# Attention and mixer: the last 64 keys' scores and a quarter of each diagonal score block turned by DMA, turns queued by the slot that needs them

## The chip, the cores and the metric

The kernel runs on one core of a Trainium2 chip. The metric is device time in microseconds (us) of the whole program, the median of the runs; lower is better. PE is the matrix engine, ACT, DVE and POOL are the scalar, vector and GpSimd engines, and SP is the engine whose queue issues all DMAs here.

## What is computed

For each of 8 batches, with S = 3136 positions, D = 256 and d_qk = 64:

```
scores = (1/S) * z @ z.T                      # S x S
x      = u * (max(scores, 0)**2 @ v)          # S x D
x2     = x + (x.T @ U @ V).T                  # rank 32
out    = x2 + max(x2 @ w_ch1, 0) @ w_ch2      # hidden 1024
```

Scores come from z with itself, so the score matrix is symmetric. The kernel works in bf16 with sums in float32.

## The kernel before

**Tiles and groups.** The 3136 positions are 24 full tiles of 128 (NF) and a tail of 64. Four tiles make a group (GT = 4, GW = 512 columns); a batch has 6 full groups (NQ) and the tail as a seventh "group" of 64 (NG = 7). `zzTs[b]` holds z transposed, twice, in the upper and the lower 64 rows, so that a score matmul contracts over 64 rows and two matmuls run side by side, one in each half of the array's rows. Nearly all matmuls come in such pairs (`pair`, line 164, called at line 169).

**Score blocks.** `blocks[b, g, J]` is a tile of 128 keys x 4 key tiles x 512 query columns: the squared, rectified scores of key group J against query group g. It is made by two "jobs" (h = 0 and 1), each a pair of 512-column matmuls (`score_pairs`, line 359), one rectification of 1024 columns (`rectify`, lines 327 to 336, on ACT or DVE, whichever the planner thinks free first) and one square on DVE (line 325). Only blocks with J >= g are made so. A block with J < g is the transpose of another one: `issue_turn` (line 346) has a DMA turn it from SBUF to SBUF (line 351, a "turn"). In batch 0 some blocks are made twice instead of turned (`made_twice`: g up to FIRST = 3, or J = g - 1). Twenty block buffers (NBLK) are shared by score blocks, turned blocks, hidden activations and some loads; `take_block` and `give_block` hand them round.

**The last 64 keys.** The 64 keys of the tail against the 512 queries of two groups are one more job, "last" (three a batch): a pair of 512-column matmuls, a rectification and a square into `last_sb`, which `av_end` (line 609) uses as the last weights of an attention sum. The opposite piece, all keys against the 64 tail queries, is made by `score_small` (line 426) into `attn_small`, in the slot of the batch's last full group, and used by `av_small` (line 562).

**Slots.** The program is one list of 56 slots t = b * 7 + g (the loop at line 1104). In slot t PE sums attention for (b, g) over its six blocks in the order J = 0 to 5 (`av_stream`), makes the scores of later slots (`todo`, line 1083; the jobs of a group are made one slot ahead, those of a new batch over three slots), and does the mixer for the group of seven slots before: `u2_unit` (line 672, the rank-32 part), the turn of x into `u2T` by DMA (`x_turn`, line 631, DMA at line 634), and, one slot later, the hidden layer (`ch1_part`, line 770, reading `u2T`; `ch2_stream`, line 812).

**The planner.** The order of all instructions is written out at build time. A modelled clock (`clock`, in units of a pair of 256 columns) advances with the matmuls, and `free_at` holds when ACT, DVE and SP are thought to be free. `held` is a list of actions with due times; `run_held` (line 114) runs those that are due. A finished square puts a block's turn into `ready_turns`; whenever SP is thought free (`free_at["sp"] <= now`) and no first group's x waits (`urgent`), the turn with the smallest (J, b, g) is issued. Each DMA books time on SP: 34 units a block turn, 15/512 a KB for a plain transfer, 17/256 for a turned one.

All DMAs stand in SP's one queue, in order. `lhs` (line 512) is what an attention matmul asks for its weights: a block made directly is read in its own layout, a turned block in another; if a turn isn't issued yet, it is issued there.

Of the kernel before, what the change touches and what calls it, by code (L numbers as in the profile page):

```python
# [9 lines left out]
BF16 = mybir.dt.bfloat16  # L10
# [8 lines left out]
def kernel(  # L19
# [79 lines left out]
    unturned = {}  # L99
    ready_turns = []  # L100
    urgent = []

    def book(eng, ready, cost):
        free_at[eng] = max(free_at[eng], ready) + cost
# [21 lines left out]
    def pe(cost):  # L126
        clock[0] += cost
# [192 lines left out]
    def half(zzT, jj, c0, n):  # L320
        return zzT.rearrange("p t c -> p (t c)")[jj * dqk : (jj + 1) * dqk, c0 : c0 + n]

    def square(a, cost=6.3):
        book("dve", clock[0], cost)
        nc.vector.tensor_tensor(out=a, in0=a, in1=a, op=ALU.mult)  # L325

    def rectify(dst, src):

        ready = clock[0] + 3
        if max(free_at["dve"], ready) + 8 < max(free_at["act"], ready):  # L330
            nc.vector.tensor_scalar(  # L331
                out=dst, in0=src, scalar1=scale, scalar2=0.0, op0=ALU.mult, op1=ALU.max
            )
            return book("dve", ready, 11.2)
        nc.scalar.activation(out=dst, in_=src, func=AF.Relu, scale=scale)  # L335
        return book("act", ready, 8.7)

# [5 lines left out]
    def made_twice(b, g, J):  # L343
        return b == 0 and (g <= FIRST or J == g - 1)

    def issue_turn(e):
# [4 lines left out]
        nc.sync.dma_start_transpose(  # L351
            out=blocks[b, J, g][1].rearrange("p j (q c) -> p (j q) c", c=P),
            in_=src[1].rearrange("p j c -> p (j c)"),
        )
        book("sp", clock[0], 34)
        if unturned.pop(src[0]):
            free_blocks.append(src[0])

    def score_pairs(jobs):

        made = []
        for b, g, job in jobs:
            zzT = zzTs[b]
            k, ps = take_ps()
            if job == "last":
# [4 lines left out]
            pair(  # L370
                k,
                [
                    (
                        jj,
                        jj,
                        dict(
                            out=ps[:, jj, :],
                            lhsT=half(zzT, jj, keys[jj] * P, P),
                            rhs=half(zzT, jj, cols[jj], GW),
                            start=True,  # L380
                            stop=True,
                        ),
                    )
                    for jj in range(2)
                ],
                GW,
            )
            if job == "last":
                lasts[b, g // 2] = pool.tile([P, 2, GW], BF16, name="last_sb")
                made.append((lasts[b, g // 2], k, ps, None, None))  # L390
                continue
            if h == 0:
                blocks[b, g, J] = take_block()
            made.append(
                (
                    blocks[b, g, J][1][:, 2 * h : 2 * h + 2, :],
                    k,
                    ps,
                    (J, g, b) if h == 1 and J > g and not made_twice(b, J, g) else None,
                    (b, g, J),  # L400
                )
            )
        return made

    def score_finish(made):
        for dst, k, ps, turn, key in made:
            if turn:
# [12 lines left out]
            hold(done, finish)  # L420

    def score_burst(jobs):
        score_finish(score_pairs(jobs))


    def score_small(b, g):
        zzT = zzTs[b]
# [6 lines left out]
        for p0 in range(0, npair, per):  # L434
            n = min(per, npair - p0)
            pk, ps = take_ps()
            for k in range(n):
                pair(
                    pk,
                    [  # L440
                        (
                            jj,
                            jj,
                            dict(
                                out=ps[:, jj, k * gw : (k + 1) * gw],
                                lhsT=half(zzT, jj, (2 * (p0 + k) + jj) * P, P),
                                rhs=half(zzT, jj, g0, gw),
                                start=(k == 0),
                                stop=(k == n - 1 and (jj == 1 or p0 + n < npair)),
                            ),  # L450
                        )
                        for jj in range(2)
                    ],
                    gw,
                )
            made.append((p0, n, pk, ps))
# [54 lines left out]
    def av_stream(b, g, box):  # L511
        def lhs(h, q, jt):
            jb, j = divmod(jt, GT)
            while (b, jb) not in v_cast:
                if spare and not b:
                    spare.pop(0)()
                else:
                    run_held(min(h[0] for h in held))
            while (b, g, jb) not in blocks:
                if (g, jb, b) in ready_turns:  # L520
                    issue_turn((g, jb, b))
                else:
                    run_held(min(h[0] for h in held))
            t = blocks[b, g, jb][1]
            if jb >= g or made_twice(b, g, jb):
                while squared.get((b, g, jb), 0) < 2:
                    run_held(min(h[0] for h in held))
                return t[h, j, q * P : (q + 1) * P]

            return t.rearrange("p a c -> p (a c)")[h, (q * GT + j) * P : (q * GT + j + 1) * P]  # L530
# [31 lines left out]
    def av_small(b, g):  # L562
# [3 lines left out]
        for jt in range(NT):  # L566
            c = jt % 2
            for h in range(2):
                nc.tensor.matmul(  # L569
                    out=ps[c * hp : c * hp + rows, h, :D],  # L570
                    lhsT=smalls[b][h * hp : (h + 1) * hp, jt, :],
                    rhs=v_bfs[b][h * hp : (h + 1) * hp, jt, :],
                    start=(jt < 2),
                    stop=(jt >= NT - 2),
                    tile_position=(h * hp, c * hp),
                )
# [31 lines left out]

    def av_end(b, g, box):

        last = lasts[b, g // 2]
        for a in range(2):
            pair(
                box["k"],
# [2 lines left out]
                    a,  # L617
                    lambda h, q: dict(
                        out=four(box["ps"])[:, q, :],
                        lhsT=last[h, g % 2, q * P : (q + 1) * P],  # L620
                        rhs=v_bfs[b][h, NF, :],
                        start=False,
                        stop=(a == 1),
# [460 lines left out]
    for b in range(B):  # L1084
        for g in range(NQ):
# [7 lines left out]
                todo[t + 1] += new[12:] if b == 1 else []  # L1093
            elif b == 0 and g == 0:
                todo[0] += new[4:]
            else:
                todo[t] += new

# [3 lines left out]

    direct = (B - 1, 0)
    for t in range(n_items):
        att = items[t]
        u2i = items[t - NG] if t >= NG else None
        mix = items[t - NG - 1] if t > NG else None
# [166 lines left out]
```

## Time and profile before

| what | value |
|---|---|
| median of 3 runs | 1004.55 us (1003.33 to 1005.26) |
| the profiled execution | 1002.76 us, its span 1001.0 us |
| granted TensorE clock | 1.000 |
| PE, DVE, ACT busy | 984.9, 655.9, 520.3 us |
| q1, the DMA queue: share of 16 engines | 77.1% |
| HBM read, written | 62.56, 25.69 MB |

The span runs from the first to the last instruction. A busy time is the time in which the engine executes at least one instruction. In a group's row, "x" stands before the count, then come the busy time in us, the mean ns of one, the idle time of the engine just before these instructions and what ended it. In a row of waits stand who waited, for whom, the total in us, how often and the longest. In a timeline row stand the start in us, the length, the engine, the line and the operation, and a count. SPq is SP's queue; its DMA rows tell how long SP took to issue.

### The profile page before, as it was taken

To read this page: it belongs to the slowest core of one execution; us is meant where nothing else is said; L and a number is where in the kernel's file an instruction comes from. 1 tells how busy PE (TensorE), PEld (TensorE's weight loads), DVE (VectorE), ACT (ScalarE), POOL (GpSimd) and SP (SyncE) were. 2 spreads that over 40 slices of the span, in tenths; PEclk is the share of its full clock that TensorE was granted. 3 is DMA by queue.
4 is the path that set the end of the run, shared out by engine and by line. 5 is a ranking of instruction groups with operands and counts; after the bars stand their busy time and mean duration, and the time that the engine had idled before them with its cause. 6 is when DMAs were issued, how large, how long until landed. Compare 5 with 4: busy or idle time off the path is not lost.

```text
span 1001.0 us, 35345 instructions
## 1 busy us (share of the span) xinstructions
PE 984.9 (98%) x16179; PEld 820.1 (82%) x16179; DVE 655.9 (66%) x822; ACT 520.3 (52%) x597; POOL 16.6 (2%) x24
## 2 busy tenths in 40 slices
PE   6999999999999999999999999999999999999997
PEld 4898888877888788887888878888888877787776
DVE  6986856668566776666856677566775667653453
ACT  6896843457335473345643465435653356522453
POOL 4100000000000000000000000000000000000000
PEclk9999999999999999999999999999999999999999
DMA  8997898978886799877897789976889586863142
GB/s 260 197 252 177 188 182 182 196 164 190 168 205 137 177 174 183 191 129 183 157 217 166 141 179 176 198 170 139 182 186 194 142 170 143 154 126 89 45 104 95
DMA packets 337061, 167.84 MB, mean 168 GB/s; under 512 B 312336, under 2 KB 315408, under 8 KB 336912
## 3 DMA queue, kind: packets, MB, share of 16 engines
q1 hardware_dynamic: 336912, 165.59, 77.1%
q8 instruction: 126, 2.06, 0.9%
q14 instruction: 23, 0.19, 0.1%
HBM read 62.56 MB, written 25.69 MB: 88 GB/s over the span
## 4 chain that ended last, share of the span: by engine, by line
PE 94%; DVE 3%; ACT 2%; issue 0%; DMA 0%; POOLq 0%; ACTq 0%
PE ps L169 92%; DVE blk L325 1%; PE ps L569 1%; ACT blk L810 1%; PE ps L646 1%; DVE out_sb L719 1%; ACT blk L335 1%; PE ps L861 0%; DMA blk<-in_z_dram 0%; DVE blk L331 0%; DVE blk L847 0%; DVE blk L1065 0%; DVE x_bf L602 0%; PE ps L306 0%; ACT zzT L315 0%
## 5 line engine op out<-in xcount | busy, mean ns | idle before, releaser
L169 PEld LDWEIGHTS <-blk 64*128 64x128 bf16 x12288 | 647.6, 94 | 123.6 <-POOLq L159 8.7
L169 PE MATMUL ps<-v_bf,blk 64*128 64x256 bf16 x9216 | 620.4, 269 | 3.3 <-DVE blk L325 2.8
L335 ACT ACTIVATE blk<-ps 128x1024 bf16<-128x1024 f32 x334 | 333.1, 1027 | 330.3 <-PE ps L169 328.5
L325 DVE TENSOR_TENSOR blk<-blk 128x1024 bf16<-128x1024 bf16 x352 | 237.3, 700 | 34.1 <-ACT blk L335 33.3
L169 PE MATMUL ps<-u2T,w_bf 64*128 64x512 bf16 (+1 forms) x1792 | 240.7, 349 | 0.7
L807 DVE TENSOR_SCALAR blk<-ps 128x1024 bf16<-128x1024 f32 (+1 forms) x114 | 132.1, 1159 | 96.1 <-PE ps L169 95.2
L169 PE MATMUL ps<-w_bf,blk 64*128 64x256 bf16 x3072 | 194.1, 269 | 0.2
L169 PE MATMUL ps<-zzT 64*128 64x512 bf16 (+1 forms) x944 | 144.9, 341 | 2.3 <-ACT zzT L315 1.7
L810 ACT ACTIVATE blk<-ps 128x1024 bf16<-128x1024 f32 (+1 forms) x110 | 93.4, 859 | 82.7 <-PE ps L169 75.2
L169 PEld LDWEIGHTS <-w_bf 64*128 64x128 bf16 x1792 | 95.8, 94 | 27.4 <-POOLq L159 3.0
L602 DVE TENSOR_TENSOR x_bf<-ps,u_sb 128x1024 bf16<-128x1024 f32 x48 | 58.7, 1222 | 62.0 <-PE ps L169 61.9
L719 DVE TENSOR_TENSOR out_sb<-ps,x_bf 128x1024 f32<-128x1024 f32 (+1 forms) x49 | 54.2, 1107 | 51.1 <-PE ps L169 50.8
L847 DVE TENSOR_TENSOR out_sb<-ps,out_sb 128x1024 f32<-128x1024 f32 x42 | 51.3, 1222 | 18.3 <-PE ps L169 18.3
L169 PEld LDWEIGHTS <-zzT 64*128 64x128 bf16 x944 | 46.1, 95 | 8.4 <-issue 2.6
L335 ACT ACTIVATE last_sb<-ps 128x1024 bf16<-128x1024 f32 x23 | 23.6, 1024 | 28.4 <-PE ps L169 28.4
L169 PE MATMUL ps<-t_sb,V_bf 64*128 64x256 bf16 x200 | 21.1, 269 | 0.0
L331 DVE TENSOR_SCALAR blk<-ps 128x1024 bf16<-128x1024 f32 x14 | 17.1, 1224 | 5.6 <-PE ps L169 4.8
L191 DVE CAST v_bf<-stage 128x1024 bf16<-128x1024 f32 (+1 forms) x30 | 20.0, 670 | 0.0
L191 DVE CAST x_bf<-out_sb 128x1024 bf16<-128x1024 f32 x28 | 19.3, 690 | 0.5
L169 PE MATMUL ps<-v_bf,last_sb 64*128 64x256 bf16 x192 | 18.8, 269 | 0.0
L847 DVE TENSOR_TENSOR blk<-ps,blk 128x1024 f32<-128x1024 f32 x6 | 7.3, 1225 | 16.0 <-PE ps L169 15.9
L588 ACT COPY u_sb<-ps 64x512 f32<-64x512 f32 x8 | 4.7, 582 | 23.9 <-PE ps L569 23.9
(68 smaller groups left out, 255.7 us busy)
## 6 DMA issues: line engine op xcount, KB each, us to landing
u_sb<-in_u_dram SPq DMA_DIRECT2D x48, 512.0 KB, 5.1
stage<-in_v_dram SPq DMA_DIRECT2D x42, 512.0 KB, 6.0
out_dram<-out_sb SPq DMA_DIRECT2D x42, 512.0 KB, 3.1
stage<-in_z_dram SPq DMA_DIRECT2D x7, 512.0 KB, 5.4
blk<-in_v_dram SPq DMA_DIRECT2D x6, 512.0 KB, 6.2
out_dram<-blk SPq DMA_DIRECT2D x6, 512.0 KB, 2.6
blk<-in_moe_w_ch_dram SPq DMA_DIRECT2D x4, 512.0 KB, 4.9
stage<-in_z_dram SPq DMA_DIRECT2D x7, 256.0 KB, 5.7
```

What stands on the lines that cost most here:

```text
L169: ins = nc.tensor.matmul(**args)
L191: nc.vector.tensor_copy(out=out, in_=in_)
L325: nc.vector.tensor_tensor(out=a, in0=a, in1=a, op=ALU.mult)
L331: nc.vector.tensor_scalar(out=dst, in0=src, scalar1=scale, scalar2=0.0, op0=ALU.mult, op1=ALU.max)
L335: nc.scalar.activation(out=dst, in_=src, func=AF.Relu, scale=scale)
L569: nc.tensor.matmul(out=ps[c * hp : c * hp + rows, h, :D], lhsT=smalls[b][h * hp : (h + 1) * hp, jt, :], rhs=v_bfs[b][h * hp : (h + 1) * hp ...
L602: nc.vector.tensor_tensor(out=xs[b, g][:rows, :n, :], in0=four(box["ps"])[:rows, :n, :], in1=u_sbs[b, g][:rows, :n, :], op=ALU.mult,)
L646: nc.tensor.matmul(out=pt[c * R : (c + 1) * R, 0, :D], lhsT=U_bf[:rows, it, :], rhs=xs[b, g][:rows, q, :], start=(it < NREP), stop=(it + N ...
L719: nc.vector.tensor_tensor(out=o[:rows, :n, :], in0=four(ps)[:rows, :n, :], in1=x, op=ALU.add)
L807: nc.vector.tensor_single_scalar(out=r, in_=ps[:, :, :gw], scalar=0.0, op=ALU.max)
L810: nc.scalar.activation(out=r, in_=ps[:, :, :gw], func=AF.Relu)
L847: nc.vector.tensor_tensor(out=o, in0=acc, in1=o, op=ALU.add)
```

## The change

1. **Last keys by DMA.** For batches 1 to 7 the "last" jobs go. Instead `score_small` for batch b runs one batch earlier (in slot 5 of batch b - 1; for batch 0 in slot 4), and at the start of the batch's first slot `last_turn` turns the first 24 tiles of `attn_small` (128 x 1536) into `last_sb` (128 x 12 x 128) with one DMA. `place_of` permutes the key tiles in `attn_small` within a group so that the two halves of rows of `last_sb` hold the query tiles that they are used for. `last_sb` has one buffer in place of two. Batch 0 keeps its three "last" jobs; those of groups 2 and 4 move one slot later.
2. **A quarter of diagonal blocks by DMA.** For blocks with J = g (in batch 0 only for g = 4 and 5) the second job is made for the second 256 query columns alone, and a DMA turns the missing quarter (128 x 512) out of the first job's half, within the same block. `in_split` finds the pieces in the new layout, and `lhs` asks for the quarter turn before the weights that need it are read. The new DMA is queued as a turn is.
3. **The order and the figures of turns.** `ready_turns` is sorted by the slot that needs the block (`needed`), and a turn that is needed in this slot or the next may be issued up to 30 units before SP is thought free. The booked figures shrink: 30 units a block turn, 12/512 and 15/256 a KB; a half rectification is booked at 6.4 or 5.3, a half square at 3.7, a quarter turn at 12, a last turn at 26.

```diff
 def queued(kb, turned=False):
-        book("sp", clock[0], kb * (17 / 256 if turned else 15 / 512))
+        book("sp", clock[0], kb * (15 / 256 if turned else 12 / 512))
...
-        while ready_turns and free_at["sp"] <= now and not urgent:
-            issue_turn(min(ready_turns, key=lambda e: (e[0], e[2], e[1])))
+        while ready_turns and not urgent:
+            e = min(ready_turns, key=needed)
+            if free_at["sp"] > now + (30 if needed(e)[0] <= slot[0] + 1 else 0):
+                break
+            issue_turn(e)
...
+    def split(b, g, J):
+        return J == g and not (b == 0 and g <= FIRST)
...
+    def in_split(j, q):
+        if j < 2:
+            return (q // 2 * 2 + j) * hw + q % 2 * P
+        return 2 * GW + (j - 2) * hw + (q - 2) * P if q >= 2 else 3 * GW + (q * 2 + j - 2) * P
...
     def issue_turn(e):
         ready_turns.remove(e)
         J, g, b = e
         src = blocks[b, g, J]
+        if J == g:
+            nc.sync.dma_start_transpose(
+                out=flat_of(src)[:, 3 * GW :].rearrange("p (n c) -> p n c", c=P),
+                in_=flat_of(src)[:, GW : 2 * GW],
+            )
+            book("sp", clock[0], 12)
+            split_turned.add((b, g))
+            return
...
-        book("sp", clock[0], 34)
+        book("sp", clock[0], 30)
...
                 keys, cols = [J * GT + 2 * h + jj for jj in range(2)], [groups[g][0]] * 2
+                if split(b, g, J) and h:
+                    width = hw
+                    cols = [c + hw for c in cols]
...
+    def last_turn(b):
+        lasts[b] = last_tile()
+        nc.sync.dma_start_transpose(
+            out=lasts[b], in_=smalls[b][:, :NF, :].rearrange("p t c -> p (t c)")
+        )
+        book("sp", clock[0], 26)
...
+                if split(b, g, jb):
+                    while j >= 2 and q < 2 and (b, g) not in split_turned:
+                        if (g, g, b) in ready_turns:
+                            issue_turn((g, g, b))
+                        else:
+                            run_held(min(h[0] for h in held))
+                    x = in_split(j, q)
+                    return t.rearrange("p a c -> p (a c)")[h, x : x + P]
...
-        if g % 2 == 0:
+        if g % 2 == 0 and b == 0:
             j.append((b, g, "last"))
...
+        if g_now == 0 and t:
+            last_turn(att[0])
...
-        if av and g_now == NQ - 1:
-            qm.append((55, 2, False, lambda: score_small(att[0], NQ)))
+        if av and t == NQ - 2:
+            qm.append((55, 2, False, lambda: score_small(0, NQ)))
+        if av and g_now == NQ - 1 and b_next < B:
+            qm.append((55, 2, False, lambda: score_small(b_next, NQ)))
```

More of the change, by code (lines that the diff above doesn't have):

```diff
@@ L101, with needed @@
     urgent = []
+    slot = [0]
+    def needed(e):
+        J, g, b = e
+        return b * NG + J, g
     def book(eng, ready, cost):
@@ L325, in square, with rectify @@
         nc.vector.tensor_tensor(out=a, in0=a, in1=a, op=ALU.mult)
-    def rectify(dst, src):
+    def rectify(dst, src, part=1):
         ready = clock[0] + 3
-        if max(free_at["dve"], ready) + 8 < max(free_at["act"], ready):
+        if max(free_at["dve"], ready) + 8 * part < max(free_at["act"], ready):
             nc.vector.tensor_scalar(
@@ L376, in score_pairs @@
                         dict(
-                            out=ps[:, jj, :],
+                            out=ps[:, jj, :width],
                             lhsT=half(zzT, jj, keys[jj] * P, P),
-                            rhs=half(zzT, jj, cols[jj], GW),
+                            rhs=half(zzT, jj, cols[jj], width),
                             start=True,
@@ L385, in score_pairs @@
                 ],
-                GW,
+                width,
             )
             if job == "last":
-                lasts[b, g // 2] = pool.tile([P, 2, GW], BF16, name="last_sb")
+                flat = last_tile().rearrange("p n c -> p (n c)")
+                lasts[b, g // 2] = flat[:, : 2 * GW].rearrange("p (a c) -> p a c", c=GW)
                 made.append((lasts[b, g // 2], k, ps, None, None))
@@ L393, in score_pairs @@
                 blocks[b, g, J] = take_block()
+            if split(b, g, J):
+                made.append((flat_of(blocks[b, g, J]), k, ps, h, (b, g, J)))
+                continue
             made.append(
@@ L406, in score_finish @@
         for dst, k, ps, turn, key in made:
+            if key and split(*key):
+                score_finish_split(dst, k, ps, turn, key)
+                continue
             if turn:
@@ L420, in score_finish, with score_finish_split, finish, place_of @@
             hold(done, finish)
+    def score_finish_split(flat, k, ps, h, key):
+        if h:
+            done = rectify(
+                flat[:, 2 * GW : 3 * GW].rearrange("p (j c) -> p j c", c=hw), ps[:, :, :hw], 0.5
+            )
+            a, cost = flat[:, 2 * GW : 3 * GW], 3.7
+        else:
+            done = rectify(
+                flat[:, : 2 * GW].rearrange("p (w j c) -> p j w c", w=2, j=2),
+                ps.rearrange("p j (w c) -> p j w c", w=2),
+            )
+            a, cost = flat[:, : 2 * GW], 6.3
+        ps_free[k] = done
+        def finish():
+            square(a, cost)
+            squared[key] = squared.get(key, 0) + 1
+            if not h:
+                b, g, J = key
+                hold(clock[0] + 7, lambda: ready_turns.append((J, g, b)))
+        hold(done, finish)
     def score_burst(jobs):
         score_finish(score_pairs(jobs))
+    def place_of(jt):
+        if jt == NF:
+            return jt
+        return jt // GT * GT + (0, 2, 1, 3)[jt % GT]
+    def last_tile():
+        return pool.tile([P, NF // 2, P], BF16, name="last_sb", bufs=1)
+    def last_turn(b):
+        lasts[b] = last_tile()
+        nc.sync.dma_start_transpose(
+            out=lasts[b], in_=smalls[b][:, :NF, :].rearrange("p t c -> p (t c)")
+        )
+        book("sp", clock[0], 26)
     def score_small(b, g):
@@ L445, in score_small @@
                                 out=ps[:, jj, k * gw : (k + 1) * gw],
-                                lhsT=half(zzT, jj, (2 * (p0 + k) + jj) * P, P),
+                                lhsT=half(zzT, jj, place_of(2 * (p0 + k) + jj) * P, P),
                                 rhs=half(zzT, jj, g0, gw),
@@ L609, in av_end, with last @@
     def av_end(b, g, box):
-        last = lasts[b, g // 2]
+        def last(h, q):
+            if b:
+                return lasts[b][h, 2 * g + q % 2, :]
+            return lasts[b, g // 2][h, g % 2, q * P : (q + 1) * P]
         for a in range(2):
@@ L1095 @@
                 todo[0] += new[4:]
+            elif b == 0 and g and g % 2 == 0:
+                todo[t] += new[:-1]
+                todo[t + 1] += new[-1:]
             else:
@@ L1104 @@
     for t in range(n_items):
+        slot[0] = t
         att = items[t]
```

14 lines of the change are left out of this document (10 added, 4 removed).

## The prediction

> **What bounds the kernel now.** I read the page first: how long PE is busy, and what the chain that ended last is made of.
>
> ```profile
> span 1001.0 us, 35345 instructions
> ...
> PE 984.9 (98%) x16179; PEld 820.1 (82%) x16179; DVE 655.9 (66%) x822; ACT 520.3 (52%) x597; POOL 16.6 (2%) x24
> ...
> PE 94%; DVE 3%; ACT 2%; issue 0%; DMA 0%; POOLq 0%; ACTq 0%
> ```
>
> PE is busy in 98% of the span, and no DMA stands in the chain. Busy matmuls are pipelined and could hide gaps, so next come PE's own waits and the busy time of two whole batches (columns: stretch, its length, PE, PEld, DVE, ACT, POOL, clock, DMA share, GB/s).
>
> ```profile
> PE ps L306 <- ACT z_bf L220: 4.1, 1, 4.1
> PE ps L169 <- DVE blk L325: 2.8, 4, 0.9
> PE ps L169 <- ACT zzT L315: 1.7, 2, 1.1
> ...
> ```
>
> ```profile
> 475.20:597.10 121.90, 121.69 (x2019) 102.78 (x2017) 81.93 (x102) 61.03 (x72) 0.00 (x0) 1.00 0.85 173
> 597.10:719.00 121.90, 121.69 (x2019) 102.78 (x2017) 81.95 (x102) 61.04 (x71) 0.00 (x0) 1.00 0.83 173
> ```
>
> The longest wait, 4.1 us, comes once (transposing the first z), and no row of that view names a DMA. A middle batch takes 121.9 us with PE idle 0.2 us, at the full clock. ACT has half of it free and DVE a third. So a batch lasts as long as its matmuls do, and the question is whether a matmul taken out gives back its time and whether the DMAs that replace it arrive before PE asks.
>
> What a pair of matmuls (two halves of the rows, side by side) costs is read from starts in PE's timeline, not from the 269 ns that the page gives for one.
>
> ```profile
> 426.06 2.25 PE L169 MATMUL ps<-v_bf,blk 64*128 64x256 bf16 x38
> 428.14 0.40 PE L169 MATMUL ps<-zzT 64*128 64x512 bf16 x2
> 428.35 0.61 PE L169 MATMUL ps<-u2T,w_bf 64*128 64x512 bf16 x4
> 428.79 0.61 PE L169 MATMUL ps<-v_bf,blk 64*128 64x256 bf16 x8
> ```
>
> 19 pairs of 256 columns go from 426.06 to 428.14: 2.08 / 19 = 0.1095 us a pair. The score pair of 512 columns lasts 0.21, the two pairs behind it 0.44 / 2 = 0.22: 0.215 us a pair. Time goes by columns.
>
> **The change part by part.** The counts come from the code and are checked against the groups:
>
> ```profile
> L169 PEld LDWEIGHTS <-blk 64*128 64x128 bf16 x12288 | 647.6, 94 | 123.6 <-POOLq L159 8.7 <-DVE blk L325 4.4 <-issue 3.7
> ...
> L169 PE MATMUL ps<-zzT 64*128 64x512 bf16 x752 | 140.7, 380 | 2.3 <-ACT zzT L315 1.7
> ...
> L335 ACT ACTIVATE last_sb<-ps 128x1024 bf16<-128x1024 f32 x23 | 23.6, 1024 | 28.4 <-PE ps L169 28.4
> ```
>
> 752 matmuls are 376 score pairs: 45 in each of batches 1 to 7, 61 in batch 0, of which 24 (three a batch; 23 rectified on ACT, one on DVE) are "last" jobs.
>
> (a) *Last jobs.* 21 of the 24 go (batch 0 keeps three): 21 x 0.215 = 4.5 us of PE. With each goes 1.02 us of ACT and a square on DVE, both beside PE, worth nothing here.
>
> (b) *Diagonal blocks.* Their second score pair shrinks from 512 to 256 columns: 6 x 7 blocks and 2 of batch 0, so 44 x (0.215 - 0.1095) = 4.6 us. Rectifying and squaring half as much is again beside PE. The 88 weight loads of these pairs stay. If loads set the pace, (b) would give nothing; but two loads of 94 ns belong to each 0.1095 us pair, so they already run side by side under the matmuls, and I take the whole 4.6. [...]
>
> (a) + (b) = 9.1 us off PE.
>
> (c) *The small scores one batch earlier* (`score_small` for batch b+1 in slot 5 of batch b): the same matmuls and ACT work elsewhere; nothing. Their key tiles are only permuted (`place_of`); nothing.
>
> (d) *New DMAs.* 44 quarter turns (512 columns) and 7 turns of the last keys (1536 columns) join SP's one queue. The nearest rows are the 2048-column block turn and the 1024-column turn of x (first numbers: SP's issue in ns; then issue to landing):
>
> ```profile
> L351 SPq DMA_TRANSPOSE blk<-blk x112: 1629/2834/6921, 21.9 to 894.9; - x112
> ```
> ```profile
> DMA to landing us min/median/max: 4.2/5.2/10.6
> ```
> ```profile
> L634 SPq DMA_TRANSPOSE u2T<-x_bf x55: 1159/1253/2222, 105.2 to 979.4; - x55
> ```
> ```profile
> DMA to landing us min/median/max: 2.3/3.3/5.2
> ```
>
> A quarter turn so costs about 1.2 us of issue, a last turn 1.2 to 2.8. SP has room: it spends far more waiting for data than the 44 x 1.2 + 7 x 2 = 67 us added.
>
> ```profile
> SPq L351 <- PE ps L169: 199.7, 84, 6.0
> SPq L849 <- DVE out_sb L847: 154.4, 48, 8.2
> ```
>
> The engines' share of 0.83 to 0.85 a batch rises: 6 x 512 + 1536 columns beside some 15 x 2048 + 6 x 1024 + 3200 turned now (40,064 columns of 256 bytes, 10.3 MB of the 173 GB/s x 121.9 us = 21.1 MB that a batch moves) is 11% more turning, so 0.88 or, if turning takes nearly all of that time, 0.94. That is room on average; what matters is who stands behind the new DMAs. Block turns are not read for a slot or more, so they can slip. The turns of x (u2T, line 634) are read within some 6 to 10 us, and two places need a look.
>
> *At the start of a batch* the listing of the changed kernel's SP instructions reads: store, u, six loads of z and tails, last turn, quarter turn, u2T of the batch before's first group. Before, nothing stood between the tails and u2T. Two such places now (SP's timeline, PE's first use, landing):
>
> ```profile
> 467.98 1.23 SPq L205 DMA_DIRECT2D stage<-in_v_dram  x2
> 472.22 1.27 SPq L634 DMA_TRANSPOSE u2T<-x_bf  x1
> ```
> ```profile
> DMA to landing us min/median/max: 5.2/5.2/5.2
> ```
> ```profile
> 478.60 0.60 PE L169 MATMUL ps<-u2T,w_bf 64*128 64x512 bf16 x4
> ```
> ```profile
> 594.13 1.25 SPq L634 DMA_TRANSPOSE u2T<-x_bf  x1
> ```
> ```profile
> DMA to landing us min/median/max: 3.3/3.3/3.3
> ```
> ```profile
> 600.51 0.59 PE L169 MATMUL ps<-u2T,w_bf 64*128 64x512 bf16 x4
> ```
>
> The spare time is 478.60 - 472.22 - 5.2 = 1.2 us in the one, 600.51 - 594.13 - 3.3 = 3.1 in the other. SP is free from 469.21 and waits 3.0 us for x; the new turns' issue of 2.4 to 4.0 us nearly fits there. On the DMA engines they are one block turn's worth (2048 columns): by the medians 5.2 - 3.3 = 1.9 us per 1024, so up to 3.8; by the minimum 4.2 against that median, 0.9, so 1.8. Part of it falls into free engines:
>
> ```profile
> 464.50:471.00 6.50, 6.50 (x133) 5.36 (x124) 5.07 (x8) 4.51 (x7) 0.00 (x0) 1.00 0.88 293
> 471.00:473.00 2.00, 2.00 (x46) 1.78 (x42) 1.82 (x4) 1.16 (x3) 0.00 (x0) 1.00 0.21 55
> ```
>
> A share of 0.21 over 2.0 us leaves 1.6, so u2T slips by 0.2 to 2.2 us. Against that, the listing puts about 0.6 us more of matmuls between making u2 and its use, and one DVE instruction fewer ahead of x's cast:
>
> ```profile
> 467.26 1.22 DVE L331 TENSOR_SCALAR blk<-ps 128x1024 bf16<-128x1024 f32 x1
> ```
>
> So the wait is from nothing to 2.2 - 0.6 - 1.2 = 0.4 us at a tight place; if none of the 3.8 were hidden, it would be 2.0. I take 0.2 on average (the free 1.6 us is measured at just that spot): 7 x 0.2 = 1.4 us. The last turn itself and the quarter are read 0.6 us earlier and 1.6 us later than u2T in the listing but queued ahead of it; no wait. Behind a late u2T on PE stands everything, as its queue is in order, so such a wait is a loss in full. [...]
>
> *Later in a batch* one quarter turn more stands ahead of u2T. The tightest place there:
>
> ```profile
> 369.50 1.26 SPq L634 DMA_TRANSPOSE u2T<-x_bf  x1
> ```
> ```profile
> 376.77 0.61 PE L169 MATMUL ps<-u2T,w_bf 64*128 64x512 bf16 x4
> ```
>
> 7.3 us less a landing of 3.3 to 5.2 leaves 2.1 to 4.0; a quarter costs 1.2 (issue). Hidden.
>
> (e) *Order and figures of the planner.* 112 block turns before and after; sorted by need, and those needed within a slot may go out up to 30 planner units (30 x 0.11 = 3.3 us) early. The listing shows at most one turn more ahead of any u2T in middle batches; bound 0 to 1 us once or twice in batch 0, where loads crowd the queue. I take 0.
>
> **Sum.** Profiled execution: 1002.76 us, span 1001.0 and 1.8 around it. 1002.76 - 9.1 + 1.4 = 995.1. The median of the runs shown, 1004.55, lies 1.8 above the profiled one; the forecast for a median is 1004.55 - 7.7 = **996.8 us**.
>
> **Rivals.**
> *R1, late u2T, and slower.* If the new turns slip u2T by their whole 3.8 us, each batch start waits 3.8 - (1.2 to 3.1), mean 1.65 us; seven of them 11.6: 1004.55 - 9.1 + 11.6 = 1007.1. It decides against the change once the mean wait is over 9.1 / 7 = 1.3 us. For it: these places have the least spare time, and one landing of 5.2. Against: the 3.0 us in which SP waits there and the share of 0.21.
> *R2, half late:* the same place with waits of 0.6 to 1.1 us: 1004.55 - 9.1 + 4.2 to 7.7 = 999.7 to 1003.1.
> *R3, columns do not come back:* the weight loads hold the pace, so (b) gives nothing; 1004.55 - 4.5 + 1.4 = 1001.5. Against: the pair starts.
> *R4, no effect:* PE stalls move to another wait, such as a block turn delayed through a batch; 1004.5. Against: no DMA releases PE anywhere now.
>
> **How the numbers follow.** Forecast (995 to 999): 0.62. R1: 0.09. R2: 0.16. R3: 0.08. R4: 0.05. About 0.2% (2 us) is what a measurement of this kernel can tell from no change. Faster by more than that, below 1002.5: the forecast, most of R2 and R3, 0.84. Within 0.2%: R4 and a little of R2, 0.07. Slower: R1, 0.09. The range starts where no wait comes and the runs' spread (1003.33 to 1005.26) helps by 0.9: 1004.55 - 9.1 - 0.9 = 994.5. It reaches up to 1002.0, through R3 and most of R2.
>
> **What would show it.** Right: matmuls 42 fewer, a middle batch of about 120.6 to 120.9 us (121.9 less 3 x 0.215 and 6 x 0.1055) with PE still busy all through; still no DMA among PE's waits, or u2T with some tenths. Wrong: a row of PE or PEld waiting for u2T, blk or last_sb by DMA with over 9 us in all (R1); pairs of 256 score columns that start 0.2 us apart (R3); batches of 121.9 us with PE's waits spread (R4).

## The result and the profile after

| | before | after |
|---|---|---|
| median (4 runs each) | 1004.23 us (1003.33 to 1005.26) | 993.32 us (991.87 to 994.57) |
| ratio | | 0.9895, 95% interval 0.9882 to 0.9907 |
| the profiled execution | 1002.76 us | 994.29 us, its span 992.5 us |

The change takes 10.9 us off; 7.7 were forecast, and 993.3 lies under the forecast range, which began at 994.5. First the page of the kernel after: its head, the DMA queue and the engines' shares of the chain that ended last.

```profile
span 992.5 us, 35366 instructions
...
PE 973.9 (98%) x16137; PEld 781.0 (79%) x16137; DVE 618.2 (62%) x793; ACT 491.4 (50%) x584; POOL 17.3 (2%) x24
...
q1 hardware_dynamic: 371824, 174.12, 86.8%
...
PE 96%; DMA 1%; DVE 1%; ACT 1%; issue 0%; POOL 0%; SPq 0%; POOLq 0%; ACTq 0%
```

42 matmuls are gone, as forecast, and the queue's share rose from 77.1% to 86.8%. DVE and ACT held 5% of the chain before and hold 2% now. PE's own waits after (us in total, times, longest):

```profile
PE ps L315 <- POOL z_bf L229: 3.2, 1, 3.2
PE ps L178 <- DVE blk L348: 1.8, 2, 0.9
PE ps L178 <- ACT v_bf L198: 1.8, 1, 1.8
...
PE ps L178 <- DMA u2T<-x_bf: 0.3, 1, 0.3
```

The forecast seven waits for u2T are one of 0.3 us. A wait of 1.8 us for a cast of v on ACT is new (before: 0.5, on DVE). Next a middle batch (window of one batch: length, PE, PEld, DVE, ACT, POOL, clock, DMA share, GB/s) and, from the chain of waits of each kernel, the 25 matmuls of t1 (`t1_all`), which come once a batch and so mark its stretch:

```profile
342.30:462.40 120.10, 120.10 (x2017) 96.08 (x2013) 76.35 (x98) 57.21 (x70) 0.00 (x0) 1.00 0.94 186
```

```profile
99.28 0.99 PE ps L646 x25
220.24 0.98 PE ps L646 x25
342.15 0.98 PE ps L646 x25
...
829.82 0.98 PE ps L646 x25
942.86 0.98 PE ps L646 x25
```

```profile
100.96 0.98 PE ps L742 x25
221.74 0.98 PE ps L742 x25
341.84 0.98 PE ps L742 x25
461.94 0.98 PE ps L742 x25
582.04 0.98 PE ps L742 x25
702.59 0.98 PE ps L742 x25
822.69 0.98 PE ps L742 x25
934.34 0.98 PE ps L742 x25
```

The differences of these starts say where the time went:

| stretch (us) | before | after | difference |
|---|---|---|---|
| start to the first t1 | 99.28 | 100.96 | +1.68 |
| first t1 to second | 120.96 | 120.78 | -0.18 |
| the next five batches | 609.58 | 600.95 | -8.63 |
| last full stretch | 113.04 | 111.65 | -1.39 |
| to the end of the span | 58.14 | 58.16 | 0 |

The first row is the start, not the change: PE waits there for POOL's copy of the first z, 0.2 us in the kernel before and 3.2 in the kernel after, but below it is 4.0 in e8 and 0.2 in e10, which start alike, and 3.4 in e1 and 0.7 in e7, which start as the kernel after. The kernels whose PE has no long wait for a DMA before it reach the first t1 between 98.6 and 102.1 us. Without this row the profiles differ by 10.2 us; the medians differ by 10.9, and by 10.2 in e1. Of the 1.39 us of the last stretch 0.36 are 25 matmuls of small scores that now run before the first t1; three shortened pairs save 0.32 there, so the sum hardly moves. A middle batch went from 121.92 to 120.10 us: 1.82 less, where the columns taken off PE are 3 x 0.215 + 6 x 0.1055 = 1.28. So 0.54 us a batch came beside the columns, and in the first stretch nearly nothing came at all. These two, and the missing u2T waits, are what the experiments are about.

### The profile page after: what moved, and what is told of

The parts are those of the page before. It is cut to its first block, busy times and chain, and to the rows that moved or that the text cites. A ratio compares the mean times of both kernels' runs of the same rounds, so it can differ in the third digit from the quotient of the medians.

```text
span 992.5 us, 35366 instructions
## 1 busy us (share of the span) xinstructions
PE 973.9 (98%) x16137; PEld 781.0 (79%) x16137; DVE 618.2 (62%) x793; ACT 491.4 (50%) x584; POOL 17.3 (2%) x24
## 3 DMA queue, kind: packets, MB, share of 16 engines
q1 hardware_dynamic: 371824, 174.12, 86.8%
## 4 chain that ended last, share of the span: by engine, by line
PE 96%; DMA 1%; DVE 1%; ACT 1%; issue 0%; POOL 0%; SPq 0%; POOLq 0%; ACTq 0%
PE ps L178 93%; PE ps L661 1%; PE ps L742 1%; DMA blk<-in_v_dram 1%; DVE blk L348 1%; DMA u2T<-x_bf 0%; ACT blk L358 0%; PE ps L957 0%; ACT blk L906 0%; POOL z_bf L229 0%; DVE blk L354 0%; DVE blk L943 0%; DVE x_bf L694 0%; POOL v_bf L249 0%; PE ps L315 0%
## 5 line engine op out<-in xcount | busy, mean ns | idle before, releaser
L178 PEld LDWEIGHTS <-blk 64*128 64x128 bf16 x12288 | 617.2, 94 | 149.0 <-POOLq L168 7.7
L178 PE MATMUL ps<-v_bf,blk 64*128 64x256 bf16 x9216 | 612.6, 269 | 3.6 <-DVE blk L348 1.8
L358 ACT ACTIVATE blk<-ps 128x1024 bf16<-128x1024 f32 x339 | 319.6, 974 | 365.6 <-PE ps L178 354.2
L348 DVE TENSOR_TENSOR blk<-blk 128x1024 bf16<-128x1024 bf16 x352 | 226.4, 666 | 42.7 <-ACT blk L358 42.1
L903 DVE TENSOR_SCALAR blk<-ps 128x1024 bf16<-128x1024 f32 (+1 forms) x110 | 127.1, 1155 | 92.9 <-PE ps L178 92.9
L178 PE MATMUL ps<-zzT 64*128 64x512 bf16 (+2 forms) x902 | 130.2, 329 | 1.7 <-ACT zzT L324 1.7
L178 PEld LDWEIGHTS <-w_bf 64*128 64x128 bf16 x1792 | 90.5, 94 | 29.2 <-POOLq L168 4.1
L198 ACT CAST x_bf<-out_sb 128x1024 bf16<-128x1024 f32 (+1 forms) x21 | 17.3, 826 | 6.0 <-DVE out_sb L815 6.0
L354 DVE TENSOR_SCALAR blk<-ps 128x1024 bf16<-128x1024 f32 (+1 forms) x9 | 10.0, 1106 | 12.9 <-PE ps L178 12.9
L682 DVE TENSOR_TENSOR u_sb<-ps,u_sb 64x512 f32<-64x512 f32 x8 | 5.5, 682 | 17.1 <-ACT u_sb L680 17.1
L198 ACT CAST v_bf<-stage 128x1024 bf16<-128x1024 f32 x15 | 15.6, 1040 | 0.0
```

Source lines behind the costliest of these rows:

```text
L178: ins = nc.tensor.matmul(**args)
L198: nc.scalar.copy(out=out, in_=in_)
L354: nc.vector.tensor_scalar(out=dst, in0=src, scalar1=scale, scalar2=0.0, op0=ALU.mult, op1=ALU.max)
L903: nc.vector.tensor_single_scalar(out=r, in_=ps[:, :, :gw], scalar=0.0, op=ALU.max)
```

## The experiments

Each kernel was timed beside the kernel before on the same chip; "middle batch" is the distance of t1 starts.

| kernel | median us | ratio (95%) | middle batch |
|---|---|---|---|
| e1 the change again | 993.78 | 0.9904 (0.9890 to 0.9919) | 120.10 |
| e2 part 1 alone | 1005.76 | 1.0025 (1.0015 to 1.0035) | 120.73 |
| e3 part 2 alone | 1018.23 | 1.0149 (1.0127 to 1.0171) | 121.00 |
| e4 part 3 alone | 1003.78 | 1.0001 (0.9990 to 1.0012) | 121.92 |
| e5 parts 1 and 2 | 1057.64 | 1.0541 (1.0525 to 1.0558) | 127.3 to 135.7 |
| e6 all, old figures | 994.65 | 0.9910 (0.9894 to 0.9927) | 120.1 to 121.6 |
| e7 all, no allowance | 992.86 | 0.9893 (0.9878 to 0.9909) | 120.10 |
| e8 before, last jobs' ACT and DVE work cut | 1004.65 | 1.0015 (1.0005 to 1.0026) | 121.92 |
| e9 before, last jobs 16 columns wide | 1000.89 | 0.9974 (0.9963 to 0.9984) | 121.53 |
| e10 before, last jobs left out | 997.70 | 0.9944 (0.9928 to 0.9961) | 120.73 |
| e11 all, a second last turn | 1001.76 | 0.9983 (0.9964 to 1.0003) | 120.8 to 124.4 |
| e12 all, early last turn, cast on DVE | 994.48 | 0.9911 (0.9893 to 0.9929) | 120.1 to 121.0 |
| e13 all, cast on DVE | 991.56 | 0.9884 (0.9867 to 0.9900) | 120.10, once 120.48 |
| e14 all, early last turn | 995.22 | 0.9912 (0.9896 to 0.9928) | 120.1 to 120.6 |

### The parts one by one (e1 to e4)

e1 is the changed kernel once more. e2, e3 and e4 each keep one part of the diff and undo the other two.

> The changed kernel once more, on the chip of the next three. Theory A (the surplus over the columns is steady: about 0.5 us a middle batch of PE waits on ACT and DVE that went): middle batches of 120.1 us again, total 992 to 994.5, and any difference to the first profile lies before the end of batch 0 (first loads). Rival B (the surplus is the spread of runs): a middle batch of 120.6 to 120.9 or a total over 995.

> Only the last keys by DMA; diagonal blocks whole, turns in the old order with the old figures. By columns 21 x 0.215 = 4.5 us, a middle batch 121.9 - 0.65 = 121.25. Theory A: ACT's queue at the end of slot 5 (a score, a hidden and a last rectification behind one another, 0.25 us of PE wait a batch) goes with the last job, so a middle batch of about 121.0 and a total 5.5 to 6.5 below before. Rival B: 121.25 and 4.5 below. If u2T at the batch start is late: 121.4 or more.

> Only the diagonal quarter by DMA; last keys on PE, turns in the old order with the old figures. By columns 44 x 0.1055 = 4.6 us, a middle batch 121.9 - 0.63 = 121.27. Theory A: no more than that, or up to 0.3 us a batch more if the wait for DVE before u2's sum goes with it. Rival R3 (weight loads hold the pace): a middle batch of 121.9.

> Only the order of turns and the smaller figures; all matmuls as before. Theory A: a middle batch of 121.9 and the time of before within 1 us, since no DMA releases PE in either kernel. Rival C (the surplus of 0.5 us a batch comes from another order of instructions): a middle batch of 121.3 to 121.5 and a total 2.5 to 4 us below before.

No part alone makes the kernel faster: +1.8, +14.3 and -0.2 us against 1003.93, while all three give -10.2. For e2 and e3 4.5 us or more under the kernel before were expected. In the middle batches both DMA parts do give their time (121.92 to 120.73 and 121.00); they lose it early. PE's waits of e2, then of e3:

```profile
PE ps L175 <- DMA blk<-blk: 6.1, 1, 6.1
```

```profile
PE ps L175 <- DMA blk<-blk: 14.2, 4, 6.8
```

These are waits for block turns, of which neither the kernel before nor the kernel after has one. The windows around e2's wait show how much more than its 6.1 us it cost:

```profile
200.00:210.00 10.00, 4.81 (x97) 3.96 (x93) 4.20 (x6) 4.52 (x9) 0.00 (x0) 0.92 1.10 170
210.00:214.00 4.00, 3.12 (x28) 2.13 (x30) 0.00 (x0) 1.02 (x1) 0.00 (x0) 0.50 0.06 12
214.00:218.00 4.00, 4.00 (x60) 2.98 (x56) 2.19 (x3) 1.02 (x1) 0.00 (x0) 0.85 0.01 4
218.00:222.00 4.00, 4.00 (x70) 3.16 (x66) 2.19 (x3) 0.08 (x1) 0.00 (x0) 1.00 0.71 131
```

While PE waits, the DMA engines are full (share 1.10 from 200 to 210 us); when it goes on, the clock granted is 0.50, then 0.85. The stretch from the first t1 to the second took 129.5 us, 8.3 to 8.9 more than in e10 and e7, which have no such wait. Part 2 alone pays this three times (waits of 2.3, 4.7 and 6.8 us). Part 3 alone changes nothing, as the forecast said of it; but with it the waits are gone.

### What in part 3 does it (e5 to e7)

e5 has both DMA parts without part 3. e6 keeps the new sort and the allowance and takes the old figures:

```diff
-book("sp", clock[0], kb * (15 / 256 if turned else 12 / 512))
+book("sp", clock[0], kb * (17 / 256 if turned else 15 / 512))
...
-book("sp", clock[0], 30)
+book("sp", clock[0], 34)
```

e7 keeps the figures and drops the allowance:

```diff
-if free_at["sp"] > now + (30 if needed(e)[0] <= slot[0] + 1 else 0):
+if free_at["sp"] > now:
```

The new sort can be judged from the program: with the old sort key in the changed kernel, every engine's instructions come out in the same order.

> Both DMA parts with the old order and figures of turns (part 3 undone). Theory A (the order and figures keep block turns in time): with the old figures the planner thinks SP busy and leaves 12 of the 112 block turns, of batches 1 to 6, until the attention of the very slot that needs them asks for them; with the whole change it leaves none. The part-1-only kernel left one such turn and lost 6.1 us of wait and some 3 us of lower clock in its batch; the part-2-only kernel left three and lost 14.2 us of wait. So 12 give 40 to 90 us of PE waiting for blk by DMA and a median of 1030 to 1085, with batches 1 to 4 the worst. Rival B (parts 1 and 2 help each other, the order is worth nothing, as it was alone): 992 to 996 and no row of PE waiting for blk by DMA.

> The whole change, but with the old booked figures (34 units a block turn, 17/256 and 15/512 a KB); the new sort and the 30 units of allowance stay. Theory A by planner's state: one block turn, (batch 1, group 4, key group 5), is left until its own slot asks for it, so one wait of some 4 to 7 us and 2 to 5 us of lower clock in batch 1: 999 to 1005, middle batches 120.1. Rival (any turn issued before its slot is fine, the one late turn hides in the stream): 992 to 996.

> The whole change without the allowance of 30 units (a turn is issued only when SP is thought free); the smaller figures stay. Theory A: no block turn is left until its slot, so no row of PE waiting for blk by DMA and 993.8 (992 to 996), as the whole change. Rival C (the allowance is what keeps turns in time): one or more waits of 4 us and up, over 998.

e5, PE's waits and the clock:

```profile
PE ps L175 <- DMA blk<-blk: 44.1, 12, 6.7
```

```profile
core 0: 1054.9 us, clock 0.979
```

44.1 us of waits and, at a mean clock of 0.979, some 20 us of slower matmuls make the 64 us between e5 and the whole change. e7 runs as the whole change does. e6 is 1.8 us slower than e7 on the same chip, with waits for u2T (2.0 us in its profile) and none for a block turn. So the smaller figures alone are enough (e7), and so are the allowance and the new sort together (e6). The planner's own clock, read while the program is written out, shows why. When it issues the turn of (batch 1, group 4, key group 5), which slot 12 needs:

| kernel | issued at (planner's units) | in slot | PE waits for a block turn |
|---|---|---|---|
| before | 1634 | 11 | no |
| after | 1530 | 11 | no |
| e7 no allowance | 1563 | 11 | no |
| e6 old figures | 1720 | 12 | no |
| e6 with the old sort | 1784 | 12 | not timed |
| e5 parts 1 and 2 | 1784 | 12 | yes |
| e2 part 1 alone | 1794 | 12 | yes |

With the old figures and more DMAs booked, the planner thinks SP busy and holds ready turns back until the slot's own matmuls ask for them; the turn then still has to be issued behind others and to land (block turns of the kernel after, medians: 2.8 us of issue, 5.5 us from issue to landing). e6 leaves one turn to its slot and yet PE doesn't wait for it (994.65): I had expected 999 to 1005, and the rival was right. So the limit isn't the slot, but how late in it the turn goes out: by the allowance and the new sort it goes 64 units earlier than in e5, some 7 us at 0.11 us a unit. The allowance without the new sort would not do it: that program issues the turn when e5 does and leaves five block turns to the slots that need them. With the smaller figures the sort is worth nothing; under the old ones it is needed.

### The surplus of 0.54 us a batch (e8 to e10)

Theory D was PE standing behind ACT's and DVE's queues. e8 keeps every matmul of the kernel before, and in batches 1 to 7 rectifies and squares 32 of a last job's 1024 columns:

```diff
             if job == "last":
+                if b:
+                    lasts[b, g // 2] = zeros
+                    made.append((pool.tile([P, 2, 16], BF16, name="strip"), k, ps, None, None))
+                    continue
                 lasts[b, g // 2] = pool.tile([P, 2, GW], BF16, name="last_sb")
...
-            done = rectify(dst, ps)
+            done = rectify(dst, ps if dst.shape[-1] == GW else ps[:, :, :16])
```

e9 narrows the pair of matmuls as well (16 columns in place of 512); e10 leaves the jobs out. All three leave the last 64 keys out of the attention of batches 1 to 7, which takes zeros for them.

> The kernel before, with the matmuls of all last jobs kept, but in batches 1 to 7 only 32 of each job's 1024 columns are rectified and squared (into a strip that nobody reads; the attention of these batches takes zeros for the last 64 keys). PE's instructions and their order stay. Theory D (the surplus of 0.5 us a batch over the columns that part 1 takes off PE was PE standing behind ACT's and DVE's queues): middle batch 121.92 goes to 121.3 to 121.5 with no column taken off PE; median 3 to 4 us under the kernel before, about 1000.5. Rival E (the pairs that part 1 takes away simply cost PE more than their 0.215 us): middle batch stays 121.9 and the median within 1 us of the kernel before.

> The kernel before; in batches 1 to 7 a last job's pair of matmuls is 16 columns wide in place of 512, its rectification and square are 32 columns in place of 1024, and the attention takes zeros for the last 64 keys. The job still takes one of the four PSUM buffers. Theory F (the surplus was PE waiting for a PSUM buffer, because each last job takes one): the columns saved before such a wait only make it longer, so a middle batch comes to 121.4 to 121.8 and the median to 2 to 4 us under the kernel before. Rival E (a last pair costs PE some 0.4 us by itself): 120.7 to 120.8 a middle batch, median 995 to 997.

> The kernel before with the last jobs of batches 1 to 7 left out altogether (matmuls, rectification, square, and so no PSUM buffer taken) and no DMA in their place; the attention takes zeros for the last 64 keys. Theories E and F both: 120.7 a middle batch, as in the kernel with part 1 alone (columns 0.645, surplus 0.54). Were it 121.3, the surplus would come from the order that the new DMA brings and not from the job's being gone. No late block turn is expected, as no DMA is added: median 995 to 997.5.

e8 refutes theory D: the batch stays at 121.92 us, with PE busy 121.70 of it, although ACT is down from 61.03 to 58.57 us and DVE from 81.93 to 80.40.

```profile
345.09:467.01 121.92, 121.70 (x2023) 102.80 (x2019) 80.40 (x102) 58.57 (x72) 0.00 (x0) 1.00 0.83 173
```

What is left of a last job in e8 is its pair of matmuls and the PSUM buffer that the pair takes, one of four. The timeline of the kernel before shows what that does at the end of a batch (start, length, engine, operation, count):

```profile
333.20 1.02 ACT L810 ACTIVATE blk<-ps 128x1024 bf16<-128x1024 f32 x1
...
333.79 0.39 PE L169 MATMUL ps<-zzT 64*128 64x512 bf16 x2
...
334.22 1.02 ACT L335 ACTIVATE last_sb<-ps 128x1024 bf16<-128x1024 f32 x1
334.27 0.82 PE L169 MATMUL ps<-u2T,w_bf 64*128 64x512 bf16 x6
```

The last pair starts at 333.79 and takes a buffer; the next pair could start 0.215 us later, at 334.00, but starts at 334.27, 0.05 after the activation that empties an older buffer ends (333.20 + 1.02). PE lost 0.27 us there, and counts as busy for 0.18 of it, since the pair's row, whose end is modelled, lasts 0.39 us and not 0.215; no row of its waits named it. A second place of this kind comes 30 us later:

```profile
364.38 1.23 DVE L719 TENSOR_TENSOR out_sb<-ps,x_bf 128x1024 f32<-128x1024 f32 x1
364.83 0.71 PE L169 MATMUL ps<-v_bf,blk 64*128 64x256 bf16 x10
365.66 0.39 PE L169 MATMUL ps<-zzT 64*128 64x512 bf16 x2
```

Five pairs of 256 columns take 0.55 us, so the score pair could start at 365.38; it starts at 365.66, 0.05 after the DVE operation that empties a PSUM buffer ends. That is 0.28 us more. Each of the five middle batches of the kernel before has these two waits, 0.55 us together, which is the surplus. In the kernel after neither is left. Where the first was, PE runs through, and the chain stays on PE:

```profile
452.54 2.98 PE L178 MATMUL ps<-u2T,w_bf 64*128 64x512 bf16 x26
```

```profile
352.56 89.80 PE ps L178 x1460
442.36 0.01 PE ps L542
442.36 15.10 PE ps L178 x229
```

e9 tells the buffer from the columns. Two of its three pairs give back nearly all of their 0.215 us, which is the 0.39 that the batch gains. The third, at the end of the batch, gives back nothing: although it is 16 columns wide, the next pair starts 0.47 us after it, where the kernel before has 0.48 (333.79 to 334.27). The wait now comes into view, since the shorter matmuls' row of 0.18 us no longer covers it; line 817 of e9 is line 810 of the kernel before.

```profile
455.19 0.18 PE L171 MATMUL ps<-zzT 64*128 64x16 bf16 x2
455.66 0.39 PE L171 MATMUL ps<-u2T,w_bf 64*128 64x512 bf16 x2 [0.30 <-ACT blk L817]
```

```profile
PE ps L171 <- ACT blk L817: 1.8, 6, 0.3
```

e10, where no buffer is taken, has 120.73 us to the hundredth, as e2 has: 0.645 us of columns and 0.545 beside them, and neither wait. At the end of the batch its matmuls stand in the order of the kernel before, with the last pair gone, and run through:

```profile
451.99 3.21 PE L171 MATMUL ps<-u2T,w_bf 64*128 64x512 bf16 x28
```

Its median, 997.70 us, lies 0.2 above what was expected. Part 2 alone brings 0.28 beside its columns: there the wait of 0.28 is gone and the one of 0.27 stays. So both parts together bring 0.54, not 0.82, as they remove the same two waits. For the wait of 0.27 the buffer of the last pair is the cause that e9 and e10 show. The wait of 0.28 stands behind no last pair; it goes in e3 too, which keeps all last jobs, and in e3 and e10 PE's matmuls come in another order at this place. Whether the buffers or the order remove it, no run tells apart.

### How late u2T is, and a wait for a cast (e11 to e14)

e11 doubles the suspected delay; e12 takes it away and moves the cast that PE waits for; e13 and e14 do one of the two each.

```diff
 last_turn(att[0])
+nc.sync.dma_start_transpose(
+    out=pool.tile([P, 10, P], BF16, name="again", bufs=1),
+    in_=smalls[att[0]][:, :20, :].rearrange("p t c -> p (t c)"),
+)
```

```diff
-if g_now == 0 and t:
-    last_turn(att[0])
+if g_now == NQ and b_next < B:
+    last_turn(b_next)
...
-return [lambda k=k, raw=raw: v_copy(b, k, raw, by_cast(GT * D))]
+return [lambda k=k, raw=raw: v_copy(b, k, raw, on_dve_cast if b == 1 else by_cast(GT * D))]
```

> The whole change with a second turn of the last keys' scores (20 of the 24 tiles, 1280 columns) right behind the first, into a tile that nobody reads, so ahead of the quarter turn and u2T at each batch start. Theory R1' (the queue ahead of u2T has a few tenths to 1.3 us of spare time and then every us counts): some 2 us of issue and 1 to 2 us of transfer more, so PE waits for u2T by DMA 6 or 7 times, 0.7 to 3 us each, 6 to 18 us in all, median 1000 to 1012. Rival (the 3 us in which SP waits for x hide it): under 1 us in all, 993 to 995.

> The whole change with the turn of the last keys issued one slot earlier (in the tail slot of the batch before, so no longer between the z loads and u2T) and the casts of batch 1's v on DVE in place of the planner's choice. If the spare time at u2T is what the traces show, no row of PE waiting for u2T by DMA; if the 1.8 us in which PE waits for a cast of v by ACT in batch 1's first slots is the ACT queue, that row goes too: median 990.5 to 993. Rival (the wait moves to the next instruction of the queue, as PE has no room behind): 993 to 994.5.

> The whole change with only the casts of batch 1's v put on DVE; the last turn stays in its place. If that cast was worth the 1.1 us by which the first batch's stretch shrank in the run with both edits, the stretch takes 119.7 us here too, and the median is 992.0 to 993.2. If the cast's shift of the planner's order made the u2T waits, rows of PE waiting for u2T by DMA sum to over 1 us; otherwise to 0.5 us or less.

> The whole change with only the turn of the last keys issued in the tail slot of the batch before. If its new place is what made the u2T waits (it pushes the block turn behind it into the way of the tail's u2T), PE waits for u2T by DMA 3 to 5 times, 1 to 2 us in all, none of them at the first u2T of a batch; median 993.5 to 995. If the cast made them: no such row, 993 to 994.

The tightest place of the kernel after first, SP's queue and PE's first use of u2T:

```profile
587.33 2.45 SPq L505 DMA_TRANSPOSE last_sb<-attn_small  x1
589.89 2.18 SPq L376 DMA_TRANSPOSE blk<-blk  x1
592.17 1.26 SPq L730 DMA_TRANSPOSE u2T<-x_bf  x1
```

```profile
596.86 0.60 PE L178 MATMUL ps<-u2T,w_bf 64*128 64x512 bf16 x4 [0.29 <-DMA u2T<-x_bf]
```

The two turns issue in 4.6 us and u2T lands 4.6 after its issue began: this is rival R1's place, and 0.29 us over. With the second turn in e11 it is over in most batches:

```profile
PE ps L178 <- DMA u2T<-x_bf: 7.9, 5, 2.4
```

The second turn took 3.15 us to issue at this place:

```profile
594.24 3.15 SPq L1239 DMA_TRANSPOSE again<-attn_small  x1
```

So some 3 us more of queue bring waits of up to 2.4, and 8 us on the median: the spare time was there, but only just, and R1 was a question of size, not of mechanism. Moving the last turn away gains nothing that the runs can show: e12's median is what the rival expected, PE still waits for u2T four times (1.3 us in all), once at the first u2T of a batch (0.2 us) and three times elsewhere; e14, with the move alone, has one such wait of 0.3 us in its profile, with runs from 991.9 to 997.6. What brings the spread of e14 stays open.

The cast on DVE removes the 1.8 us wait for ACT. In e12 the first stretch then takes 119.70 us, 1.1 less than in the kernel after; in e13, where 119.7 was expected, it takes 120.55, as a u2T wait of 1.1 us stands in its place. e13's median of 991.56 is the lowest of all, but its interval overlaps that of e1 and its profile is shorter only at the start, before the first t1 (98.7 us against 101.2 in e1); that it beats the change is not shown.

## Why the prediction was right and where it was wrong

- **Columns (a, b): right.** 0.215 and 0.1055 us a pair hold: 42 fewer matmuls, a middle batch 1.28 us shorter by columns, R3 (columns do not come back) refuted by e2 and e3. The batch shrank by 1.82 us; without the two waits of 0.55 that is 1.27.
- **"With each goes 1.02 us of ACT and a square on DVE, both beside PE, worth nothing here": the step that failed.** The sum took nothing but columns for a job that goes. The sentence is true of ACT's and DVE's work (e8: the batch stays at 121.92 us), but a job also takes a PSUM buffer and a place in the order of matmuls, and that had a price that no wait showed: two hidden waits, 0.54 us a batch, 2.7 us in the five middle batches. The sign named for a right forecast, a middle batch of 120.6 to 120.9 us, did not come; it took 120.10. What the profile did show was the 5% of DVE and ACT in the chain that ended last, which I read and passed over because PE's waits named nothing.
- **(c) Small scores earlier: right.** e2, which has them, and e10, which has not, both give 120.73 us.
- **(d) New DMAs, +1.4 us: wrong by size.** One wait of 0.29 us, 0.45 us on the batch (120.55 against 120.10). The spare time was worth more, and the tightest place was where it was put. PE waited for one of the seven u2T at batch starts, where I had taken 0.2 us on average.
- **(e) Order of the planner, 0: right of the part alone (e4), wrong of the whole.** I looked at u2T and at middle batches of the changed kernel, where no turn is late. From batch 1 on, the old order with the new DMAs leaves twelve turns too late, and the change would have cost 55 us (e5). A rival for that was missing: R4 had block turns delayed, but with no price.
- **The first stretch.** Of about 1.3 us of columns 0.18 came back: PE waits 1.8 us for a cast of v on ACT, behind another cast and a rectification (1.05 and 1.04 us), where the kernel before has 0.5 for DVE. Part 3 doesn't bring it: e4 has the 0.5 for DVE. e2 and e10, both without the last jobs, have the 1.8. The prediction had no term for it.
- **Sum.** Five middle batches: 6.4 of columns + 2.7 - 0.45 = 8.6; last stretch 1.4; first 0.2: 10.2 us. Forecast: 9.1 - 1.4. So 0.95 of the 1.4 us that (d) took off didn't come, 2.7 us of hidden waits came that the sum had at nothing, and the first stretch lost most of its columns. The range began at 994.5 because I took nothing but columns and the runs' spread for its low end.

## What to carry to other kernels

Where a few buffers go round, count the buffer as part of a job's price (here a wait of 0.27 us a batch), and look at pieces of other engines in the chain of waits even when the waiting engine shows no idle time: compare starts of matmuls with what their columns take. A change that adds DMAs to a queue that a planner books must be judged together with the booked costs: parts that lose alone can win together (+1.8 and +14.3 us alone, -10.2 with part 3), and a middle batch doesn't show it: those of e2 and e3 are shorter, and the loss lies in their first batches. Moving a transfer away from one tight place can make a wait at another (e12: 0.2 us at the first u2T of a batch, 1.1 us elsewhere); measure the spare time by adding a dose before spending effort on it.

## What the hardware showed beside that

In these runs a wait of PE could be dearer than its length, since the granted clock was 0.50 for a time after it. Nine waits in e2, e3 and e5 took between 4.22 and 6.76 us, and with each the clock went to half. It stayed there for 3.4 or 6.8 us; e2's wait of 6.1 us cost 8.3 to 8.9. The longest wait in e3 ended at 342.23 us (in these rows the column before the last two is the granted clock):

```profile
340.70:347.50 6.80, 5.27 (x42) 3.12 (x44) 0.00 (x0) 1.80 (x2) 0.00 (x0) 0.50 0.23 44
347.50:351.00 3.50, 3.50 (x68) 3.06 (x64) 2.42 (x3) 0.25 (x1) 0.00 (x0) 1.00 0.02 5
```

With shorter waits it went both ways. In e5 PE waited 2.46, 1.58 and 2.51 us, up to 206.63, 210.12 and 216.88 us, and the clock stayed at 1.00:

```profile
206.00:210.00 4.00, 1.91 (x26) 1.18 (x26) 1.42 (x2) 1.02 (x1) 0.00 (x0) 1.00 0.59 128
210.00:214.00 4.00, 3.88 (x81) 3.24 (x83) 1.78 (x4) 2.57 (x4) 0.00 (x0) 1.00 0.46 85
217.00:221.00 4.00, 4.00 (x68) 3.19 (x66) 1.29 (x2) 2.05 (x2) 0.00 (x0) 1.00 0.01 4
```

Waits of 2.31 us in e3 (up to 97.07 us) and of 2.44 us in e11 (up to 725.66 us) were followed by 3.4 us at half:

```profile
98.30:101.70 3.40, 3.40 (x32) 2.05 (x28) 1.00 (x2) 0.66 (x1) 0.00 (x0) 0.50 0.92 270
```

```profile
726.80:730.20 3.40, 3.40 (x32) 2.13 (x28) 0.51 (x1) 2.39 (x3) 0.00 (x0) 0.51 1.02 189
```

So these runs show no one length of wait at which the clock falls: it fell after 2.31 and 2.44 us and stayed after 2.46 and 2.51 us, and what decides there stays open.
